# The layout of u's spectra in DRAM, the sign-flipped table, and the place of the table for the transform back

## The chip, the cores and the metric

The kernel runs on one core of a Trainium2 chip. The metric is the device time of one execution in microseconds (us), less is better. The core has five engines that run their own instruction lists and wait for each other by semaphores: TensorE (PE; its weight loads are listed as PEld), VectorE (DVE), ScalarE (ACT), GpSimd (POOL) and SyncE (SP), which here only issues transfers. Transfers between DRAM and the on-chip memory run on 16 DMA engines, whichever engine issued them.

## The reference

The whole is a conditioned layer for one sequence of 2,048 tokens and 512 channels, in float32. A vector c gives six rows of scales and shifts; a state-space convolution follows, then a token-shift mixer with an MLP.

```python
mod = (_silu(c) @ w_mod).reshape(c.shape[0], 6, 1, -1)
h = _layernorm(x, axis=-1) * (1 + ca) + sa
x = x + ga * _A_ref(h, ...)          # the convolution
h = _layernorm(x, axis=-1) * (1 + cb) + sb
x = x + gb * _B_ref(h, ...)          # token shifts and MLP

# _A_ref: taps K from the state space, then a causal convolution by a transform of length 4096
K = jnp.einsum("dn,dnl,dn->dl", Cc, P, dB).real
Kf = rfft2(pad(K)); Uf = rfft2(pad(u)); Yf = Uf * Kf
y = irfft2(Yf)[..., :L] + u * Dskip
```

The change touches the convolution alone: Uf, Kf, their product, and the first part of the transform back.

## The kernel before, in words

The work runs in three parts. The first, up to about 207 us of the profiled execution, makes the taps K (exponentials and sines on ACT, products on DVE, sums on PE) and beside it normalizes u and takes the first stage of u's transform, `u_dft` (lines 420 to 436). Each call makes 64 rows of half a spectrum for two token groups with the table `FU` as weights; ACT copies them to the tile `vs`, and SP stores them to `VU` in DRAM, 128 KB a store, in pieces of 256 floats (1 KB). There are 64 such stores.

The second part, from about 207 to 304 us, is the spectral one. `k_first` (eight rounds, with the table `FK` as moving operand) takes the first stage of the taps' transform. Then come sixteen steps, `steps` (line 1096): two halves of 256 channels (`jh`) by eight blocks of four of the 32 first-stage frequencies (`kc`). Each step has

- `load_vu` (line 638): SP loads 512 KB of VU to a tile `ld`, three steps ahead in the program; seven `ld` tiles are shared with the loads of w1 and ZT;
- `spectrum_u` (line 642): PE takes the second stage of u's transform with the table `TU`, ACT copies the result to `us`;
- `spectrum_k` (line 664): PE takes the second stage of the taps' transform, with parts of the table `T2`, and, for one of its four quarters, with the same table negated, the tile `T3`;
- `multiply` (line 685): DVE multiplies the two spectra;
- `back` (line 695): PE applies the table `Gm`, ACT copies to a tile `z` (two of them), and POOL stores z to `ZT` in DRAM, two transfers of 256 KB with 4-KB pieces.

`flip` (line 658) makes T3 on POOL: two operations for the eight frequencies that two steps need, into one of three tiles. The table `T2` stands in two tiles of sixteen frequencies, named xu in the profile, that were loaded at the end of the first part; `TU` stands in a tile named wm. Further loads stand in SP's queue among the VU loads: four of x (1 MB each), w1, FI, w2, and later the loads of ZT that the last stage of the transform back reads (`load_inv`, `inverse`). The third part, from about 304 us, is the rest of the transform back, the mixer and the MLP; PE is busy nearly throughout.

The order of each engine's work in the second part is the order in which the program's lines are written (`manual_schedule`). SP and POOL issue their transfers in that order, and an issue that has to wait holds back everything behind it on the same engine. A tile that takes the place of an older one waits for the last reader of the older one.

Of the kernel before, what the change touches and what calls it, by code (L numbers as in the profile page):

```python
# [7 lines left out]
F32 = mybir.dt.float32  # L8
# [3 lines left out]
OP = mybir.AluOpType  # L12
# [15 lines left out]
def shape_constants():  # L28
    f = lambda x: np.ascontiguousarray(x.astype(np.float32))
    k1, k2, q = np.arange(32), np.arange(64), np.arange(32)  # L30
    c2b = lambda c: np.where(c < 32, 31 - c, c)
    th = 2 * np.pi * (k1[None] + .5) * q[:, None] / 64
    W = np.stack([np.cos(th), -np.sin(th)], 1)
    Wt = W.transpose(0, 2, 1)
    FU = np.stack([np.stack([Wt, -Wt[..., ::-1]], 1), np.stack([Wt, Wt[..., ::-1]], 1)])
    FU = np.stack([FU, FU])
    FK = np.zeros((2, 2, 32, 2, 64))
    FK[:, 0, :, 0] = FK[:, 1, :, 1] = W.reshape(32, 64)
    b = c2b(np.arange(64))
    al = 2 * np.pi * b[:, None, None] * ((k1[None, :, None] + .5) / 4096 + k2[None, None, :] / 64)  # L40
    c, s = np.cos(al), np.sin(al)
    T2 = np.stack([np.stack([c, -s], 2), np.stack([s, c], 2)]).reshape(128, 32 * 128)
    be = np.arange(32) + .5
    al = 2 * np.pi * be[:, None, None] * ((k1[None, :, None] + .5) / 4096 + k2[None, None, :] / 64)
    TU = np.stack([np.cos(al), np.sin(al), np.cos(al), -np.sin(al)]).reshape(128, 32 * 64)
    al = 2 * np.pi * be[None, :] * k2[:, None] / 64
    cs = np.stack([np.cos(al), np.sin(al)], 2).reshape(64, 64)
    Gm = np.tile(np.concatenate([cs, cs], 1), (2, 1))
    sg = np.array([1.0, -1.0])[:, None]
    th = 2 * np.pi * (k1[:, None, None, None] + .5) * (sg * be[:, None, None] + 64 * q) / 4096  # L50
    FI = np.stack([np.cos(th), -sg * np.sin(th), -np.sin(th), -sg * np.cos(th)]) * (2 / 4096)
    eye = np.eye(16)
    j = np.arange(32)
    c0 = np.tile((eye[:, :, None] * (j + .5)).reshape(16, 512), (2, 1))
    C0 = np.zeros((2, 2, 32, 2, 512))
    C0[:, 0, :, 0], C0[:, 1, :, 1] = c0, c0
    C0 = C0.reshape(128, 1024)
    e1 = (eye[:, :, None] * j).reshape(16, 512)
    e2 = (eye[:, :, None] * np.ones(32)).reshape(16, 512)
    C1 = np.concatenate([e1, e1, e2, e2] * 2, 0)  # L60
    ex0 = np.concatenate([np.arange(31, -1, -1), np.arange(32, 64)])
    ex1 = np.concatenate([64 * np.arange(8), 512 * np.arange(4)])
    CE = np.concatenate([(eye[:, :, None] * ex0.reshape(2, 32)[:, None, None, :]).transpose(1, 0, 2, 3).reshape(16, -1),
                         np.zeros((16, 64 * NX1))], 1)
    CE = np.tile(CE, (8, 1))
    for u in range(4):
        CE[u * 32:u * 32 + 32, 1024 + u * 16 * NX1:1024 + (u + 1) * 16 * NX1] = \
            np.tile((eye[:, :, None] * ex1).reshape(16, -1), (2, 1))
    PA = np.zeros((2, 4, 16, 2, 2, 4, 2, 16))
    PB = np.zeros((4, 2, 16, 4, 4, 2, 4, 16))  # L70
    for e in range(16):
        for v in range(2):
            for u in range(4):
                for p in range(2):
                    PA[v, u, e, v, p, u, p, e] = 1
        for c in range(8):
            for p in range(4):
                PB[c // 2, c % 2, e, c // 4 * 2 + c % 2, p, 1 - c // 2 % 2, p, e] = 1
    return {k: f(v) for k, v in dict(
        FU=FU.reshape(128, 128), FK=FK.reshape(128, 128), T2=T2, TU=TU, G=Gm,  # L80
        FI=FI.reshape(128, 32 * 64), C0=C0, C1=C1, CE=CE, PA=PA.reshape(128, 512), PB=PB.reshape(128, 2048), ID=np.eye(128)).items()}
# [21 lines left out]
def dram(t, off, ap):  # L103
    return bass.AP(tensor=t.tensor, offset=t.offset + off, ap=ap)


def body(ctx, tc, A):
    nc = tc.nc
    V, S, P, T, Y = nc.vector, nc.scalar, nc.gpsimd, nc.tensor, nc.sync
# [7 lines left out]
    VU = dpool.tile([2, 64, 64, 256], F32, name="VU")  # L117
# [52 lines left out]
    pa12 = a12.enter_context(pool("a12"))  # L170
# [5 lines left out]
    FK = pa12.tile([128, 128], F32, name="FK")  # L176
# [8 lines left out]
    FU = ph.tile([128, 2, 64], F32, name="FU")  # L185
# [234 lines left out]
    def u_dft(b, eo):  # L420
        x = ut[b // 4]
        ps = [psu.tile([128, 512], F32, name="pu") for h in range(2)]
        for i in range(2):
            for h in range(2):
                j = slice(64 * h, 64 * h + 64)
                T.matmul(ps[h][i * 64:i * 64 + 64], FU[j, eo], x[j, b % 4 + i],  # L426
                         start=True, stop=True, skip_group_check=True)

        def evict():
            vs = uv.tile([128, 2, 512], F32, name="vs")  # L430
            for h in range(2):
                act(vs[:, h], ps[h])
                for i in range(2):
                    Y.dma_start(dram(VU, eo * 8192 + (h * 16 + b + i) * 256, [[16384, 64], [1048576, 2], [1, 256]]),
                                vs[i * 64:i * 64 + 64, h].rearrange("p (a d) -> p a d", a=2))
        later.append(evict)

# [166 lines left out]
    v0x = ExitStack()  # L604
    c2 = a2.enter_context(pool("c2"))
    TU = TU[0]
    Gm = c2.tile([128, 2, 64], F32, name="Gm")
    FI = c2.tile([128, 32, 2, 32], F32, name="FI")
    VK = [v0x.enter_context(pool("v0", side="right")).tile([128, 64, 2, 64], F32, name="VK0"),
          c2.tile([128, 64, 2, 64], F32, name="VK1")]  # L610
    ldp = a2.enter_context(pool("ldp", bufs=7))
    s2x = ExitStack()
    s2 = s2x.enter_context(pool("s2", bufs=2))
    psa = s2x.enter_context(pool("psa", bufs=2, space=PSUM))
    psb = s2x.enter_context(pool("psb", bufs=4, space=PSUM))
    kbank = lambda shape: psb.tile(shape, F32, name="pk2")
# [20 lines left out]

    def load_vu(jh, kc):
        t = vus[jh, kc] = block()
        Y.dma_start(t, dram(VU, jh * 1048576 + kc * 8 * 16384, [[256, 128], [32768, 4], [1, 256]]))  # L640

    def spectrum_u(jh, kc):
        vu = vus.pop((jh, kc))
        us = s2.tile([128, 3, 2, 256], F32, name="us")
        q = [psa.tile([128, 2, 256], F32, name="pk1") for ro in range(2)]
        for i in range(2):
            for kk in range(2):
                for ro in range(2):
                    r = slice(ro * 64, ro * 64 + 64)
                    T.matmul(q[ro][kk * 64:kk * 64 + 64, i], TU[r, kc * 4 + 2 * kk + i], vu[r, 2 * kk + i],  # L650
                             start=True, stop=True, skip_group_check=True)
        for n in range(3):
            act(us[:, n], q[n % 2])
        return us

    t3s = {}

    def flip(kc):
        t = t3s[kc] = c2.tile([128, 8, 64], F32, name="T3", bufs=3)
        for gh in range(2):  # L660
            r = slice(gh * 64, gh * 64 + 64)
            P.tensor_scalar(t[r], T2[kc // 4][r, kc % 4 * 4:kc % 4 * 4 + 8, 64 - gh * 64:128 - gh * 64], -1.0, None, op0=OP.mult)

    def spectrum_k(jh, kc):
        p = [kbank([128, 2, 2, 128]) for gh in range(2)]
        for i in range(2):
            for ro in range(2):
                for ri in range(2):
                    for kk in range(2):
                        for gh in range(2):  # L670
                            k1 = kc * 4 + 2 * kk + i
                            rows = slice(gh * 64, gh * 64 + 64)
                            w = T2[k1 // 16][rows, k1 % 16]
                            if ri == gh:
                                w = w[:, ro * 64:ro * 64 + 64]
                            elif ro == ri:
                                w = w[:, gh * 64:gh * 64 + 64]
                            else:
                                w = t3s[kc // 2 * 2][rows, k1 % 8]
                            T.matmul(p[gh][kk * 64:kk * 64 + 64, i, ro], w,  # L680
                                     VK[jh][rows, ri * 32 + k1].rearrange("p j g -> p (j g)"),
                                     start=(ri == 0), stop=(ri == 1), skip_group_check=True)
        return p
# [413 lines left out]
    with tc.manual_schedule():  # L1097
        load_vu(*steps[0])
        flip(0)
        Y.dma_start(Gm, A["G"].rearrange("p (a b) -> p a b", a=2))  # L1100
        for r in range(8):
            k_first(r)
            if r == 3:
                load_vu(*steps[1])
            if r == 6:
                load_vu(*steps[2])
        us = spectrum_u(*steps[0])
        split = None
        for n, st in enumerate(steps):
# [13 lines left out]
                us = spectrum_u(*steps[n + 1])  # L1123
            if n + 3 < 16:
                load_vu(*steps[n + 3])
            if n % 2 == 0 and n < 14:
                flip(steps[n + 2][1])
            if n in (3, 4, 6, 8):
                load_x(n - 3 if n < 5 else n // 2 - 1)
            if n == 9:  # L1130
# [171 lines left out]
```

## Time and profile before

| | |
|---|---|
| median of three runs | 689.6 us (687.0 to 690.3) |
| the profiled execution, its own time | 691.26 us |
| its span, first to last instruction | 689.5 us |
| mean granted TensorE clock | 0.989 |
| PE busy over the span | 642.6 us, 93% |
| DVE / ACT / POOL busy | 498.0 / 331.2 / 124.8 us |
| moved by the DMA engines | 86.42 MB, mean 125 GB/s |
| 16 loads of VU, 512 KB each | median 7.4 us from issue to landing |
| 30 stores of ZT by POOL, 256 KB each | median 6.2 us from issue to landing |

The profile comes from one execution. "Busy" counts the time in which an engine works, not the time in which it waits. A row `A <- B` in the waits says that A stood idle and that B ended it. The DMA share is the mean busy share of the 16 DMA engines; it can read slightly over 1 in a short window, since a packet counts where it starts. A landing is the time from a transfer's issue to its last byte.

### The profile page before, as it was taken

Reading aid. Unit: us, or ns where it says so; the run is one execution under the profiler, and the core shown is the slowest. Engines: PE = TensorE matmul, PEld = TensorE weight load, DVE = VectorE, ACT = ScalarE, POOL = GpSimd, SP = SyncE. Lnnn points to the kernel's source line nnn. Section 1 sums busy time; section 2 is a strip of 40 time slices with the busy share of each in tenths; the row PEclk is TensorE's granted clock in tenths of the full one; section 3 lists DMA queues with packets and bytes.
Section 4 is the critical chain, followed back from the end, with each engine's and each line's share of the span. In section 5 each row is a group of like instructions: output and inputs, shape, how many; then the busy total and the mean of one; then the engine's idle time right before and its main releaser. Section 6 shows DMA issues by size and latency. Waiting matters only on the chain.

```text
span 689.5 us, 16884 instructions
## 1 busy us (share of the span) xinstructions
PE 642.6 (93%) x7195; PEld 509.2 (74%) x7195; DVE 498.0 (72%) x795; ACT 331.2 (48%) x505; POOL 124.8 (18%) x236
## 2 busy tenths in 40 slices
PE   1899999999999998977998999999999999999996
PEld 0456655655569776634887889999899889898895
DVE  7899999999996887986987967464574536363522
ACT  3878988889875557432444623123131312222121
POOL 4011112112103355413741101001010000000000
PEclk9999999999999999998999999999999999999999
DMA  8603264643739997967387010020100201010001
GB/s 299 284 2 79 75 218 105 209 121 85 275 85 317 354 335 258 346 204 226 108 257 240 1 32 32 16 77 15 47 31 17 77 1 62 1 49 13 1 31 31
DMA packets 51091, 86.42 MB, mean 125 GB/s; under 512 B 4676, under 2 KB 39496, under 8 KB 48424
## 3 DMA queue, kind: packets, MB, share of 16 engines
q1 hardware_dynamic: 46712, 66.74, 30.1%
q0 software_dynamic: 3440, 17.57, 7.4%
q8 instruction: 56, 0.92, 0.6%
q10 hardware_dynamic: 864, 1.05, 0.5%
q14 instruction: 19, 0.16, 0.1%
HBM read 59.12 MB, written 32.90 MB: 133 GB/s over the span
## 4 chain that ended last, share of the span: by engine, by line
PE 70%; DVE 6%; DMA 5%; ACT 3%; POOL 2%; issue 1%; ACTq 0%; SPq 0%; DVEq 0%; POOLq 0%
PE pm L841 7%; PE pm L838 7%; PE pm L839 7%; PE xx L448 7%; PE pa L954 6%; PE pa L955 6%; PE pa L962 6%; PE kp L498 3%; DMA ZT<-z 3%; PE ph L893 2%; PE ph L895 2%; PE ph L892 2%; DMA ld<-ZT 2%; PE pu L426 2%; PE pT L803 2%; PE pk L626 2%
## 5 line engine op out<-in xcount | busy, mean ns | idle before, releaser
L115 ACT ACTIVATE gh<-pm 128x512 fp32r<-128x512 f32 (+1 forms) x48 | 26.9, 560 | 200.7 <-PE pm L841 200.7
L838 PE MATMUL pm<-nh,w3h 128*128 128x256 f32 (+1 forms) x352 | 86.6, 281 | 2.7 <-ACT nh L115 2.7
L839 PE MATMUL pm<-nh,w3l 128*128 128x256 f32 (+1 forms) x352 | 86.3, 280 | 0.1
L946 DVE TENSOR_TENSOR gl<-gf,gh 128x512 fp32r<-128x512 f32 (+1 forms) x48 | 30.8, 643 | 68.4 <-ACT gf L115 68.4
L954 PE MATMUL pa<-w4h,gh 128*128 128x512 f32 (+1 forms) x176 | 69.6, 395 | 0.0
L838 PEld LDWEIGHTS pm<-nh,w3h 128*128 128x128 f32 (+1 forms) x352 | 66.0, 187 | 4.4 <-ACT nh L115 2.9
L955 PE MATMUL pa<-w4l,gh 128*128 128x512 f32 (+1 forms) x176 | 68.9, 392 | 0.0
L839 PEld LDWEIGHTS pm<-nh,w3l 128*128 128x128 f32 (+1 forms) x352 | 65.9, 187 | 2.2 <-DVE w3l L756 0.5
L765 POOL TENSOR_TENSOR rs<-mv,eps_t 128x1 f32<-128x1 f32 (+1 forms) x39 | 11.0, 282 | 282.4 <-DVE mv L771 265.4
L841 PE MATMUL pm<-nl,w3h 128*128 128x256 f32 (+1 forms) x352 | 55.0, 278 | 0.0
L449 PE MATMUL xx<-MG,ON 64*128 64x512 f32 x160 | 48.1, 397 | 0.0
L962 PE MATMUL pa<-w4h,gl 128*128 128x512 f32 (+1 forms) x176 | 48.0, 390 | 0.0
L448 PE MATMUL xx<-MG,ON 64*128 64x512 f32 x160 | 48.0, 396 | 0.0
L841 PEld LDWEIGHTS pm<-nl,w3h 128*128 128x128 f32 (+1 forms) x352 | 47.0, 187 | 0.0
L898 DVE TENSOR_TENSOR h<-h,ph 128x512 f32<-128x512 f32 x16 | 11.0, 687 | 45.1 <-PE ph L895 45.1
L466 DVE SCALAR_TENSOR_TENSOR e<-tr,p 128x512 f32<-128x512 f32 x64 | 41.1, 684 | 1.5 <-ACT tr L115 1.5
L498 PEld LDWEIGHTS kp<-e,e 128*32 128x32 f32 x2048 | 30.1, 110 | 12.7 <-issue 7.6
L475 DVE TENSOR_TENSOR e<-tr,p 128x1024 f32<-128x1024 f32 x32 | 39.0, 1220 | 0.0
L476 DVE TENSOR_TENSOR e<-tr,m 128x1024 f32<-128x1024 f32 x32 | 39.0, 1219 | 0.0
L115 ACT ACTIVATE p<-xx 128x1024 f32<-128x1024 f32 (+1 forms) x40 | 37.5, 979 | 2.2 <-PE xx L252 1.0
L962 PEld LDWEIGHTS pa<-w4h,gl 128*128 128x128 f32 (+1 forms) x176 | 33.0, 188 | 7.3 <-DVE gl L946 0.2
L115 ACT ACTIVATE tr<-xx 128x1024 f32<-128x1024 f32 x32 | 33.0, 1030 | 9.6 <-PE xx L449 7.9
(236 smaller groups left out, 1731.6 us busy)
## 6 DMA issues: line engine op xcount, KB each, us to landing
VU<-vs SPq DMA_DIRECT2D x64, 128.0 KB, 3.7
ld<-VU SPq DMA_DIRECT2D x16, 512.0 KB, 7.4
ZT<-z POOLq DMA_DIRECT2D x30, 256.0 KB, 6.2
ld<-ZT SPq DMA_DIRECT2D x12, 512.0 KB
Dw<-in_w POOLq DMA_DIRECT2D x8, 688.0 KB, 4.7
xu<-in_u SPq DMA_DIRECT2D x4, 1024.0 KB, 8.0
KX<-in_x SPq DMA_DIRECT2D x4, 1024.0 KB, 8.0
GD<-go SPq DMA_DIRECT2D x16, 256.0 KB, 2.3
```

What stands on the lines that cost most here:

```text
L115: return S.activation(out, in_, f, bias=bias, scale=scale)
L448: T.matmul(x[:, :512], la, ma, start=(i == 0), stop=(i == len(ops) - 1))
L449: T.matmul(x[:, 512:], lb, mb, start=(i == 0), stop=(i == len(ops) - 1))
L466: V.scalar_tensor_tensor(e0[:, 1, a], tr[:, 1, 0], 1.0 - 2.0 * a, mg[:, a], op0=OP.mult, op1=OP.mult)
L475: V.tensor_mul(e0[:, 0], tr[:, 0, 0:1].to_broadcast([128, 2, 512]), mg)
L498: T.matmul(kp[32 * j:32 * j + 32, (k % 2) * 4 + g], e1[:, r, d], e0[:, r, :, d * 32:d * 32 + 32], start=(r == 0), stop=(r == 1), skip_grou ...
L838: T.matmul(p, wh[:, k, c], hi[k], start=(k == 0), stop=False)
L839: T.matmul(p, wl[:, k, c], hi[k], start=False, stop=False)
L841: T.matmul(p, wh[:, k, c], lo[k], start=False, stop=(k == 3))
L954: T.matmul(acc[i], gh[:m, e, s], W4h[:m, f], start=(f == 0), stop=False)
L955: T.matmul(acc[i], gh[:m, e, s], W4l[:m, f], start=False, stop=False)
L962: T.matmul(acc[i], gl[:m, e, s], W4h[:m, f], start=False, stop=(f == 10))
```

## The change

There are three edits.

**VU's layout.** It was [half of the channels][frequency and part][64 rows][256 channels], so that one row's neighbours in a block lay 128 KB apart, and a load took 512 pieces of 1 KB. It becomes [half][64 rows][part, frequency][256 channels]: a row's four frequencies of a block lie behind each other, and a load takes 128 pieces of 4 KB. For that the columns of the table `FU` are reordered from frequency-by-part to part-by-frequency. The store's pieces stay 1 KB; the 64 pieces of one store and half now lie behind each other. The same bytes move.

**The flipped table.** `flip` now negates one whole tile of T2 at a time, in four operations of the old size, into a T3 of all 32 frequencies that is kept; it is called twice, before the steps, and no longer in them.

**The table for the transform back.** `Gm` has no tile of its own any more: it is loaded into FK's, behind the first three VU loads in SP's queue, after the last round of `k_first`.

```diff
-    Wt = W.transpose(0, 2, 1)
-    FU = np.stack([np.stack([Wt, -Wt[..., ::-1]], 1), np.stack([Wt, Wt[..., ::-1]], 1)])
+    FU = np.stack([np.stack([W, -W[:, ::-1]], 1), np.stack([W, W[:, ::-1]], 1)])
...
-                    Y.dma_start(dram(VU, eo * 8192 + (h * 16 + b + i) * 256, [[16384, 64], [1048576, 2], [1, 256]]),
+                    Y.dma_start(dram(VU, (eo * 32 + h * 16 + b + i) * 16384, [[256, 64], [1048576, 2], [1, 256]]),
...
-    Gm = c2.tile([128, 2, 64], F32, name="Gm")
...
+    T3 = s2.tile([128, 32, 64], F32, name="T3", bufs=1)
...
     def load_vu(jh, kc):
         t = vus[jh, kc] = block()
-        Y.dma_start(t, dram(VU, jh * 1048576 + kc * 8 * 16384, [[256, 128], [32768, 4], [1, 256]]))
+        Y.dma_start(t.rearrange("p a d -> p (a d)"), dram(VU, jh * 1048576 + kc * 1024, [[8192, 2], [16384, 64], [1, 1024]]))
...
-    t3s = {}
-
-    def flip(kc):
-        t = t3s[kc] = c2.tile([128, 8, 64], F32, name="T3", bufs=3)
+    def flip(i):
         for gh in range(2):
             r = slice(gh * 64, gh * 64 + 64)
-            P.tensor_scalar(t[r], T2[kc // 4][r, kc % 4 * 4:kc % 4 * 4 + 8, 64 - gh * 64:128 - gh * 64], -1.0, None, op0=OP.mult)
+            for a in range(0, 16, 8):
+                P.tensor_scalar(T3[r, i * 16 + a:i * 16 + a + 8], T2[i][r, a:a + 8, 64 - gh * 64:128 - gh * 64], -1.0, None, op0=OP.mult)
...
-                                w = t3s[kc // 2 * 2][rows, k1 % 8]
+                                w = T3[rows, k1]
...
         load_vu(*steps[0])
         flip(0)
-        Y.dma_start(Gm, A["G"].rearrange("p (a b) -> p a b", a=2))
+        flip(1)
         for r in range(8):
             k_first(r)
             if r == 3:
                 load_vu(*steps[1])
             if r == 6:
                 load_vu(*steps[2])
+        Gm = pa12.tile([128, 2, 64], F32, name="FK")
+        Y.dma_start(Gm, A["G"].rearrange("p (a b) -> p a b", a=2))
...
-            if n % 2 == 0 and n < 14:
-                flip(steps[n + 2][1])
```

In `dram(VU, offset, pattern)` the pattern lists [step, count] from the outermost dimension to the innermost, in floats.

On SP, at the start of the spectral part, the transfers stood so before (`ld<-VU` is a VU load, `KX<-in_x` a load of x; a name behind "waits" that begins with DMAHW is an earlier transfer, PE_49 is TensorE):

```order
L1100 DMA Gm<-in_G 128x128
L640 DMA ld<-VU 128x4x256 [waits DMAHW6_49]
L640 DMA ld<-VU 128x4x256 x4
L640 DMA ld<-VU 128x4x256 [waits DMAHW3_49]
L724 DMA KX<-in_x 128x2048 [waits DMAHW4_49,PE_49]
L640 DMA ld<-VU 128x4x256 [waits DMAHW5_49,PE_49]
```

and stand so now:

```order
L639 DMA ld<-VU 128x1x1024
L639 DMA ld<-VU 128x1x1024 [waits DMAHW6_49]
L1105 DMA FK<-in_G 128x128 [waits PE_49]
L639 DMA ld<-VU 128x1x1024 x3
L639 DMA ld<-VU 128x1x1024 [waits DMAHW3_49]
L721 DMA KX<-in_x 128x2048 [waits DMAHW4_49]
```

The load of G has moved behind the third VU load and waits for TensorE; four more VU loads and the first load of x stand behind it. A VU load's shape on the tile's side is 128 rows of one run of 1,024 floats, where it was 128 rows of four runs of 256.

On POOL, in the spectral part, the table's operations (`T<-xu`) and the stores of ZT stood so before:

```order
L662 TENSOR_SCALAR T_3081<-xu 64x512 x2
L662 TENSOR_SCALAR T_3355<-xu 64x512 x2
L706 DMA ZT_61<-z 32x2x1024 x4
L662 TENSOR_SCALAR T_3500<-xu 64x512 x2
L706 DMA ZT_61<-z 32x2x1024 x4
L662 TENSOR_SCALAR T_3646<-xu 64x512 x2
```

and stand so now:

```order
L511 DMA Dw_64<-in_w 16x8192 x2
L659 TENSOR_SCALAR T_3070<-xu 64x512 x8
L703 DMA ZT_61<-z 32x2x1024 x16
L703 DMA ZT_62<-z 32x2x1024 x14
L762 TENSOR_TENSOR rs_79<-mv_78,eps_t 128x1
```

All eight operations stand ahead of the first store, and no table operation stands among the stores.

## The prediction

> **What bounds the kernel now.** I read the busy times by stretch first, to find what runs where the change acts, then the chain of waits and the waits there, then SP's queue and the DMA packets. The windows are the transform of the kernel's taps, the sixteen spectral steps, and the hand-over behind them (start and end, then busy time of PE, PEld, DVE, ACT, POOL, then TensorE clock, DMA share, GB/s):
>
> ```profile
> 213.00:224.00 11.00, 10.67 (x190) 10.56 (x190) 8.00 (x12) 8.16 (x15) 2.43 (x2) 1.00 0.91 291
> 224.00:304.00 80.00, 72.85 (x1528) 52.97 (x1526) 69.60 (x116) 45.73 (x90) 35.15 (x42) 1.00 0.91 312
> 304.00:316.00 12.00, 5.22 (x47) 2.82 (x47) 3.70 (x9) 0.34 (x1) 0.00 (x0) 0.85 0.76 231
> ```
>
> Sixteen steps in 80 us are 5.0 us a step. PE is busy 91% of that, DVE 87%, the 16 DMA engines 91%: three resources near their end together, so whatever takes a DMA engine much longer shows at once. The chain of waits names what ends last in it (start, length, what):
>
> ```profile
> 234.17 8.87 DMA ZT<-z
> 252.91 8.02 DMA ZT<-z
> 291.66 7.89 DMA ld<-ZT
> ```
>
> and the waits from 200 to 310 us (engine, line, waited for: sum, times, longest):
>
> ```profile
> ACT z L115 <- DMA ZT<-z: 8.7, 3, 4.3
> PEld pk L680 <- POOL T L662: 2.3, 3, 0.8
> PE pk L680 <- POOL T L662: 1.6, 3, 0.5
> ```
>
> Nobody waits for a VU load: `ld` has seven buffers, and SP's queue runs far ahead, as its timeline shows:
>
> ```profile
> 212.65 0.39 SPq L640 DMA_DIRECT2D ld<-VU  x1
> 213.09 1.61 SPq L1100 DMA_DIRECT2D Gm<-in_G  x1
> 214.74 5.15 SPq L640 DMA_DIRECT2D ld<-VU  x6
> 220.00 1.67 SPq L724 DMA_DIRECT2D KX<-in_x  x1
> ```
>
> What is to be priced is therefore DMA engine time. Packets, MB and share of all 16 engines, first over 217 to 225 us (VU loads alone, 1-KB packets), then 226 to 228 us (an x load, 8-KB packets), then the stage's two queues:
>
> ```profile
> DMA packets 2822, 2.82 MB, mean 352 GB/s; under 512 B 80, under 2 KB 2821, under 8 KB 2821
> q1 hardware_dynamic: 2821, 2.80, 106.2%
> ...
> DMA packets 168, 0.82 MB, mean 409 GB/s; under 512 B 6, under 2 KB 77, under 8 KB 77
> q1 hardware_dynamic: 168, 0.82, 101.5%
> ...
> q1 hardware_dynamic: 11422, 16.88, 61.8%
> q0 software_dynamic: 2400, 7.87, 28.2%
> ```
>
> A 1-KB packet costs 1.062 x 16 x 8 us / 2,741 = 50 ns on one engine (the 80 tiny ones cost next to nothing). The 8-KB window gives 1.015 x 16 x 2 / 0.82 MB = 39.6 us per MB on one engine, so 162 ns for 4 KB. The ZT stores are 4-KB packets: 0.282 x 16 x 80 us / 1,920 (7.87 MB in 4 KB) = 188 ns. A 4-KB piece of VU lies between; I take 162, since the x load is a read as the VU load is.
>
> **Over how many engines a transfer is spread.** Packets under 512 B are the end marks. The 217 to 225 window has 2,741 pieces and 80 marks, 15 for 512 pieces (its edges cut loads): 16 for each load. From 12.5 to 15.0 us four one-row loads, DS, pass, beside one POOL load that ends:
>
> ```profile
> DMA packets 196, 1.09 MB, mean 434 GB/s; under 512 B 20, under 2 KB 24, under 8 KB 105
> ```
>
> 24 - 20 = 4 pieces of 512 B are the DS rows; of the 20 marks 16 belong to the POOL load and 4 to the rows: one each. So a transfer has one mark for each engine it used, and one row uses one engine. SP's large loads and stores of before begin their pattern, on both sides, with a count that is a multiple of 16 (128, 96, 64 or 32). The changed VU load begins its DRAM side with a count of **2**: `[[8192, 2], [16384, 64], [1, 1024]]`. The 2 and the 64 cannot fold into one count of 128, as 64 x 16384 is not 8192. Two readings fit the trace: engines by the first count (two here), or by the number of pieces (128, so sixteen). The one-row loads do not part them. I take the first: a split by the first count explains each mark, and no transfer of before is seen to be split along a second count.
>
> [...]
>
> **The change part by part.**
>
> *The VU load.* On sixteen engines it costs 512 x 50 ns / 16 = 1.60 us now, and would cost 128 x 162 / 16 = 1.30 us. On two it is 64 x 162 ns = **10.4 us**, against a step of 5.0. Sixteen of them are 166 us on those two engines (at 188 ns, 193 us). It cannot hide: it is two stages long.
>
> *What shares these two engines.* SP's queue is in order on each engine, so the other loads stand between the VU loads. Ahead of the last VU load are x (4 MB), FI, w1 (1 MB each), the first four ZT loads (2 MB) and G: 8.45 million bytes, 0.53 MB an engine; at 39.6 to 46.9 us per MB (the stage's q1 row: 0.618 x 16 x 80 / 16.88) 21 to 25 us, say 22. The ZT stores come on POOL's queue, 8 packets an engine a step: 13 steps x 8 x 188 ns = 19 us. Sum: 166 + 22 + 19 = 207 us from 212.65, so the last VU load lands at about **420 us**.
>
> *What waits for it.* The last VU load feeds the matmuls that began at 293.78; the second four loads of the first ZT half (2 MB), with w2 (1 MB) ahead of them, stand behind it: 0.2 MB an engine, 9 us, and 3 us for two more steps' stores; landed at 432. Before, the matmuls that need them began at 299.59, after a wait of 1.48:
>
> ```profile
> 293.78 1.04 PE L650 MATMUL pk<-ld,wm 64*64 64x256 f32 x16
> 299.59 1.93 PE L731 MATMUL pk<-ld,FI 128*32 128x256 f32 x32 [1.48 <-DMA ld<-ZT]
> ```
>
> PE is in order, so the last step's transform back stands behind these: 432 - 299.6 = 132 us later. From there nothing reads VU, and all transfers start with 64 or more: the rest keeps its length.
>
> *The flipped table.* Sixteen POOL operations become eight, all at the start:
>
> ```profile
> L662 POOL TENSOR_SCALAR T<-xu 64x512 f32<-64x512 f32 x16 | 24.6, 1536 | 27.3 <-DMA wm<-in_TU 26.2
> ```
>
> 8 x 1.54 = 12.3 us from about 209.3 end near 222, before the first spectral step's matmuls at 225; step 0 needs the first three. The second half waits for the second T2 load, there at 212.8. PE's waits for T (2.3 and 1.6 us, the same three events) go: at most 2 us, worth nothing where PE waits for VU.
>
> *G in FK's place.* SP's queue now stops at G until the last FK matmul, at 224.4, with four VU loads and x behind it. On two engines that is covered: the three VU loads ahead last 31 us, to 244. With sixteen it is not: 1.5 MB are through by about 218.5, and the DMA engines idle 6 us, 2.1 MB at 351 GB/s that then press into a stage whose free DMA time is 0.09 x 80 = 7 us. Price there: 0 to 6 us.
>
> *VU stores and the reordered FU:* 1-KB pieces and a first count of 64 as before; only their addresses close up. Nothing waits for them but the first VU load.
>
> The sum is made against the profiled execution's own 691.3 us (span 689.5), 1.7 above the runs' median: 691.3 + 132 = 823, less 1 to 2 for the table's waits: **822 us**.
>
> **Rivals.**
>
> 1. *Sixteen engines after all, not slower.* Place: the DMA engines in the stage. 0.30 us a load off (0.11 at 188 ns), 1.8 to 4.8 over sixteen, and up to 2 for the table, with G's 6 us sunk into the free 7. Time: 685 to 688. For it: the 8.7 us ACT waits for ZT stores shrink with shorter queues. Against: the first count of 2.
> 2. *Sixteen engines, and G's wait decides.* The 2.1 MB held back meet the first ZT stores, which already take 8.87 us and hold ACT. It decides if the ZT stores' delay exceeds the 1.8 to 4.8 us saved: 691 + 6 - 3 = 694.
> 3. *Two engines, but dearer.* If the two are slowed as ZT stores are (188 ns, +27 us) and 1-KB traffic delays them more, 850 to 875. If the ZT stores and other loads slip beside the VU packets, the sum is 212.65 + 166 + 12: 795.
>
> A load decides as soon as its time exceeds the step: 20.7 us of engine time over fewer than about five engines.
>
> **How the numbers follow.** Two engines, 0.86 (0.78 within the sum's bounds, 785 to 875, with 0.08 beyond), rival 1 0.08, rival 2 0.06. A measurement of this kernel can tell 0.5%, 3.4 us, from no change. Faster: rival 1's better half and a little more, 0.06; same: the rest of it and half of rival 2, 0.07; slower: 0.87. The range 785 to 875 leaves the sixteen-engine cases out, and holds 0.78.
>
> **What would show it.** In the changed profile: VU loads landing in over 10 us, tens of them when queued; 224 to 304 at a DMA share near 0.4 or below; the chain from 224 to about 430 mostly "DMA ld<-VU"; PE, DVE and ACT idle half of each step at a pitch of 12 to 13 us; each VU load with 2 marks instead of 16; after the stage the old lengths. The forecast is wrong if these loads land in 5 to 8 us with a DMA share near 0.9; then rivals 1 and 2 part by whether SP's gap from 214 to 224 is followed by longer waits of ACT z for ZT.

## The result, and the profile after

The changed kernel takes **827.6 us** (median of four runs, 825.0 to 828.3), against 689.4 us (687.0 to 690.3) for the kernel before on the same chip: a ratio of 1.200, 95% interval 1.196 to 1.205. Its profiled execution has a span of 825.6 us, at a mean granted TensorE clock of 0.919. Times are medians of all runs, while each ratio is of the fast runs alone, which leaves out two of the twelve runs of one experiment (the doubled stores). The same bytes move, and PE, DVE and ACT run as many instructions as before; nearly all of the 138 us is waiting.

The stretches of the changed kernel's trace show where (start and end, length, then busy time of PE, PEld, DVE, ACT and POOL, TensorE clock, DMA share, GB/s):

```profile
213.00:224.00 11.00, 10.87 (x192) 10.67 (x192) 7.67 (x12) 7.86 (x15) 6.09 (x5) 1.00 0.13 48
224.00:304.00 80.00, 39.51 (x608) 29.71 (x608) 26.42 (x43) 18.03 (x34) 6.53 (x12) 0.73 0.35 108
304.00:440.00 136.00, 61.93 (x916) 38.75 (x920) 43.32 (x72) 28.53 (x55) 9.61 (x18) 0.71 0.46 139
```

From 224 to 304 us, where the kernel before ran all sixteen steps, PE is now busy for half of the time and the DMA engines for 35%. By these averages nothing is near its end, and yet the stage lasts to 440. In the first row VU loads run nearly alone, at a share of 0.13. The packets of 214 to 231 us say the same more closely (packets, MB, share of all 16 engines):

```profile
DMA packets 207, 0.87 MB, mean 51 GB/s; under 512 B 2, under 2 KB 2, under 8 KB 204
q1 hardware_dynamic: 204, 0.83, 12.1%
```

12.1% of sixteen engines is 1.94 engines. With 202 pieces of 4 KB in 17 us, a piece costs 0.121 x 16 x 17 / 202 = 163 ns on its engine, and the load moves at 51 GB/s. The end marks agree: over the whole execution, packets under 512 B fell from the first of these rows (the page of before) to the second (the page of after).

```profile
DMA packets 51091, 86.42 MB, mean 125 GB/s; under 512 B 4676, under 2 KB 39496, under 8 KB 48424
```

```profile
DMA packets 44723, 86.42 MB, mean 105 GB/s; under 512 B 4452, under 2 KB 31080, under 8 KB 42056
```

4,676 - 4,452 = 224 = 16 loads x 14: each VU load leaves 2 marks where it left 16.

The chain of waits in the stage (start, length, what) and the waits from 205 to 460 us (sum, times, longest):

```profile
253.81 39.55 DMA ld<-VU
...
295.05 37.84 DMA ld<-VU
...
392.98 18.89 DMA ld<-VU
...
439.81 0.60 ACT z L114
```

```profile
PE pk L649 <- DMA ld<-VU: 88.7, 14, 11.8
```

Three loads of VU alone make up 96 us of the chain; PE waits for fourteen of the sixteen. The last of these three lands at 411.9 and is the fifteenth load. The sixteenth landed at about 425.0, as PE's matmuls on it show (first row below). PE reaches the matmuls behind the last ZT loads at 434.57 (second row), where the kernel before reached them at 299.59:

```profile
425.15 1.98 PE L649 MATMUL pk<-ld,wm 64*64 64x256 f32 x16 [6.07 <-DMA ld<-VU]
...
434.57 2.89 PE L728 MATMUL pk<-ld,FI 128*32 128x256 f32 x32 [4.07 <-DMA ld<-ZT]
```

The copy to z behind it starts at 439.81 (the chain above); in the chain of the kernel before the same copy reads

```profile
303.75 0.60 ACT z L115
```

From there to the end of the span are 385.8 us in both kernels (825.6 - 439.8, and 689.5 - 303.75).

SP's queue holds something that the prediction had not asked about. In the timeline of its issues (start, busy time, line, what, how many), and in the summary of the loads' line (shortest, median and longest issue in ns):

```profile
212.08 10.29 SPq L639 DMA_DIRECT2D ld<-VU  x3
223.93 8.42 SPq L1105 DMA_DIRECT2D FK<-in_G  x1
232.40 32.51 SPq L639 DMA_DIRECT2D ld<-VU  x4
...
410.56 16.17 SPq L718 DMA_DIRECT2D ld<-ZT  x4
...
L639 SPq DMA_DIRECT2D ld<-VU x16: 514/3186/11854, 212.1 to 394.4; - x16
```

Before, the same summary read

```profile
L640 SPq DMA_DIRECT2D ld<-VU x16: 359/377/2106, 212.6 to 278.7; - x16
```

An issue of a VU load took 0.38 us; now the median is 3.2 us and the longest 11.9. While the two engines are behind, the issue itself takes long, and G, a 64-KB transfer, takes 8.4 us to be issued behind three of these loads.

### The profile page after: what moved, and what is told of

It reads as the page before. It is cut to its first block, busy times and chain, and to the rows that moved or that the text cites. A ratio compares the mean times of both kernels' runs of the same rounds, so it can differ in the third digit from the quotient of the medians.

```text
span 825.6 us, 16875 instructions
## 1 busy us (share of the span) xinstructions
PE 669.0 (81%) x7195; PEld 524.2 (63%) x7195; DVE 498.1 (60%) x795; ACT 332.2 (40%) x505; POOL 111.6 (14%) x228
## 2 busy tenths in 40 slices
DMA packets 44723, 86.42 MB, mean 105 GB/s; under 512 B 4452, under 2 KB 31080, under 8 KB 42056
## 4 chain that ended last, share of the span: by engine, by line
PE 56%; DMA 19%; DVE 11%; SPq 7%; ACT 3%; issue 2%; POOL 1%; ACTq 0%; DVEq 0%; POOLq 0%
DMA ld<-VU 12%; PE pm L838 6%; PE pm L836 6%; PE pm L835 6%; PE xx L447 6%; PE pa L951 5%; PE pa L952 5%; PE pa L959 5%; SPq L639 3%; PE kp L497 3%; DMA ld<-in_w 2%; DMA ld<-ZT 2%; PE ph L890 2%; PE ph L892 2%; PE ph L889 2%
## 5 line engine op out<-in xcount | busy, mean ns | idle before, releaser
L649 PE MATMUL pk<-ld,wm 64*64 64x256 f32 x256 | 30.8, 624 | 90.6 <-DMA ld<-VU 88.7
L649 PEld LDWEIGHTS pk<-ld,wm 64*64 64x64 f32 x256 | 14.1, 208 | 109.7 <-issue 108.6
L687 DVE TENSOR_TENSOR ma<-pk,us 128x512 f32<-128x512 f32 x32 | 21.9, 685 | 81.0 <-PE pk L677 81.0
L114 ACT ACTIVATE us<-pk 128x512 f32<-128x512 f32 x48 | 25.2, 599 | 93.6 <-issue 80.9
L762 POOL TENSOR_TENSOR rs<-mv,eps_t 128x1 f32<-128x1 f32 (+1 forms) x39 | 10.9, 280 | 286.2 <-DVE mv L768 265.6
L677 PEld LDWEIGHTS pk<-VK,xu 64*64 64x64 f32 x768 | 44.8, 187 | 5.1 <-issue 4.1
L448 PE MATMUL xx<-MG,ON 64*128 64x512 f32 x160 | 47.1, 389 | 0.0
L447 PE MATMUL xx<-MG,ON 64*128 64x512 f32 x160 | 47.0, 389 | 0.0
L677 PE MATMUL pk<-VK,xu 64*64 64x128 f32 x768 | 45.4, 346 | 0.0
L703 POOL DMA_DIRECT2D ZT<-z x30 | 16.1, 542 | 196.6 <-ACT z L114 196.6
```

Of the source, the lines that this page charges most:

```text
L114: return S.activation(out, in_, f, bias=bias, scale=scale)
L447: T.matmul(x[:, :512], la, ma, start=(i == 0), stop=(i == len(ops) - 1))
L448: T.matmul(x[:, 512:], lb, mb, start=(i == 0), stop=(i == len(ops) - 1))
L677: T.matmul(p[gh][kk * 64:kk * 64 + 64, i, ro], w, VK[jh][rows, ri * 32 + k1].rearrange("p j g -> p (j g)"), start=(ri == 0), stop=(ri == 1 ...
```

## The experiments

The theory: a transfer is spread over no more DMA engines than the first count of its DRAM pattern allows; a first count of 2 puts each VU load on two engines, and that is all of the loss. The rivals: the edits that move SP's queue (G's wait) or POOL's work (the whole flipped table) have a part in it; or the 4-KB pieces at their new addresses are dear by themselves. Every kernel below computes the whole output. The runs of before beside them had medians of 688.8 to 689.8 us, and each ratio is against those beside it.

### The load as two transfers, each with a first count of 64

```diff
-        Y.dma_start(t.rearrange("p a d -> p (a d)"), dram(VU, jh * 1048576 + kc * 1024, [[8192, 2], [16384, 64], [1, 1024]]))
+        for ri in range(2):
+            Y.dma_start(t[ri * 64:ri * 64 + 64].rearrange("p a d -> p (a d)"),
+                        dram(VU, jh * 1048576 + ri * 8192 + kc * 1024, [[16384, 64], [1, 1024]]))
```

> The changed kernel with each VU load made as two transfers, one for each half of the tile's partitions, so that the DRAM pattern begins with 64 instead of 2. Same bytes, same addresses, same 4-KB pieces, 32 issues instead of 16. Theory (a transfer is spread over as many DMA engines as its first count allows, 2 in the change): all sixteen engines again, the VU loads cost 1.3 to 1.5 us of all engines each, and the time falls back to 684 to 694 us. Rival (the 4-KB pieces at a 64-KB pitch in DRAM, or the load of G that holds SP's queue, cost the 136 us): these are untouched, so it stays at 815 to 830 us.

Measured: 699.8 us (698.3 to 705.9), 1.0153 of before (1.0139 to 1.0167). Same layout, same pieces, same addresses, and 128 us are gone. What changed is the first count, and that a load is now two transfers over half of the partitions each; the next experiment keeps the half loads and varies the count. But 10.5 us stay, and the expected range is missed by 6. The profiled execution was the longest of the six (705.9 us), so its trace shows more than the usual loss. The stretch of this kernel's sixteen steps, the packets of 213 to 219 us and the wait for ZT stores from 205 to 330 us:

```profile
224.00:304.00 80.00, 66.22 (x1384) 50.79 (x1380) 59.05 (x99) 38.91 (x77) 14.05 (x26) 0.96 0.98 302
...
DMA packets 397, 1.35 MB, mean 225 GB/s; under 512 B 71, under 2 KB 71, under 8 KB 394
q1 hardware_dynamic: 396, 1.34, 89.7%
...
ACT z L114 <- DMA ZT<-z: 18.4, 5, 5.5
```

The DMA engines are now full (0.98 against 0.91) and move less (302 against 312 GB/s). A 4-KB piece costs 0.897 x 16 x 6 / 325 = 265 ns, not 162 (the 71 marks are left out: in the traces of before and after the record of a mark lasts 9 ns). ACT's wait for the ZT stores has grown from 8.7 to 18.4 us.

### First counts of 4 and of 8

The 64 rows in DRAM got a gap of 4 KB after every 16 (or 8) rows, so that they no longer lie at one pitch, and each half load begins its pattern with 4 (or 8). The edit for four (VU's larger size is not shown):

```diff
...
-                    Y.dma_start(dram(VU, (eo * 32 + h * 16 + b + i) * 16384, [[256, 64], [1048576, 2], [1, 256]]),
+                    Y.dma_start(dram(VU, (eo * 32 + h * 16 + b + i) * 16384 + (eo * 32 + h * 16 + b + i) // 16 * 1024, [[256, 64], [1052672, 2], [1, 256]]),
...
-        Y.dma_start(t.rearrange("p a d -> p (a d)"), dram(VU, jh * 1048576 + kc * 1024, [[8192, 2], [16384, 64], [1, 1024]]))
+        for ri in range(2):
+            Y.dma_start(t[ri * 64:ri * 64 + 64].rearrange("p a d -> p (a d)"),
+                        dram(VU, jh * 1052672 + ri * 8192 + kc * 1024, [[263168, 4], [16384, 16], [1, 1024]]))
```

> As the kernel with half loads, but VU's rows lie in groups of 16 with 4 KB of padding behind each group, so that a half load's pattern begins with a count of 4. Theory: four engines; a load is 32 pieces an engine, 5.3 us; the last VU load lands at 212.7 + 16 x 5.3 + 41 = 338 us, the last ZT loads 12 us later, 50 us after the 299.6 of before: 735 to 750 us. Rival (the number of pieces sets the engines, 64 pieces give sixteen): the time of the half loads, 684 to 694 us.

> The same with groups of 8 rows: a half load's pattern begins with 8. Theory: eight engines, 16 pieces an engine and load, 2.6 us; the last VU load lands at about 212.7 + 42 + 41 = 296 us, with the ZT loads behind it at 307, 7 us after before: 693 to 702 us. Rival (number of pieces): 684 to 694 us.

Measured: 749.7 us with four (1.0881, 1.0852 to 1.0910), 714.3 us with eight (1.0386, 1.0338 to 1.0434). The loads' queue from 213 to 219 us, first with four, then with eight:

```profile
DMA packets 143, 0.57 MB, mean 94 GB/s; under 512 B 9, under 2 KB 9, under 8 KB 141
q1 hardware_dynamic: 141, 0.54, 24.8%
```

```profile
DMA packets 212, 0.82 MB, mean 136 GB/s; under 512 B 20, under 2 KB 20, under 8 KB 207
q1 hardware_dynamic: 210, 0.79, 44.2%
```

24.8% is 4 of 16 engines, 44.2% is 7 of 16. The end marks say it exactly. Over the whole execution the packets under 512 B are 4,452 in the changed kernel (16 loads), and with 32 half loads 4,548 with four, 4,676 with eight and 4,932 with a first count of 64. That is 4,420, and 2, 4, 8 and 16 more for each load or half load; before, with a first count of 128, it was 4,676, which is 16 for each of the sixteen loads. The windows of 213 to 219 us, whose edges cut loads, have 4.4, 6.7 and, with 64, 14.0 marks for 64 pieces. So in these runs the number of engines follows the first count of the DRAM pattern: 2, 4 and 8 engines with counts of 2, 4 and 8, sixteen with 64 and 128. The tile's side began with 128 or 64 in all these kernels, so these runs don't show what a small count there does. Four came out at the upper end of its range; eight came out 12 us above it. The rows say why. A piece costs 0.248 x 96 / 132 = 180 ns with four engines and 0.442 x 96 / 190 = 223 ns with eight, and I had taken the 162 of the full-width load. (The profiled execution with eight took 721.6 us, the longest of its four.) With these prices, which the runs gave afterwards, one sum covers the doses. An engine that carries VU pieces also carries, in each step, eight ZT pieces at 188 ns (1.5 us) and a sixteenth of the prediction's 22 us of other loads (1.4 us), 2.9 us together by this estimate:

| engines | pieces on each, per load | ns a piece | us a step, with the 2.9 | 16 x the excess over 5.0 | measured |
|---|---|---|---|---|---|
| 2 | 64 | 163 | 13.3 | +133 | +138 |
| 4 | 32 | 180 | 8.7 | +59 | +61 |
| 8 | 16 | 223 | 6.5 | +24 | +27 |
| 16, two half loads | 8 | 265 | 5.0 | 0 | +10.5 |
| 16, before | 32 of 1 KB | 50 | 4.5 | under | 0 |

The last column is the ratio less one, times the 689 us of before. The 13.3 us a step can be seen in the trace too: from the first VU load's issue to the sixteenth's landing are (425.0 - 212.1) / 16 = 13.3. The row of the half loads is the one that the sum does not give: it stands just at the step, at a DMA share of 0.98, and still costs 10 us.

### Half loads with the kernel before's layout

This raises the question whether half loads are dear by themselves. So the kernel before, with its 1-KB pieces, got its loads split in the same way and nothing else.

```diff
-        Y.dma_start(t, dram(VU, jh * 1048576 + kc * 8 * 16384, [[256, 128], [32768, 4], [1, 256]]))
+        for ri in range(2):
+            Y.dma_start(t[ri * 64:ri * 64 + 64], dram(VU, jh * 1048576 + kc * 8 * 16384 + ri * 16384, [[256, 64], [32768, 4], [1, 256]]))
```

> The kernel before with nothing changed but each VU load made as two transfers of 64 partitions, 1-KB pieces. Theory (half the partitions move at a lower rate): a 1-KB piece costs some 65 ns instead of 50, a load 2.0 us instead of 1.6, 7 us of DMA time over sixteen loads in a stage that is 91% full: 692 to 700 us. Rival (two transfers move as fast as one, and the 4-KB pieces were to blame): 688 to 691 us.

Measured: 700.2 us (696.9 to 701.5), 1.0138 (1.0119 to 1.0158), at the upper end of the range. Half loads are dear by themselves. Its two stretches, to be read beside those of the kernel before, and ACT's wait for the ZT stores from 205 to 330 us:

```profile
213.00:224.00 11.00, 11.00 (x196) 10.88 (x200) 7.61 (x11) 7.87 (x14) 1.13 (x1) 1.00 0.98 223
224.00:304.00 80.00, 66.78 (x1450) 51.16 (x1451) 62.11 (x103) 42.15 (x82) 33.67 (x40) 0.98 1.01 300
...
ACT z L115 <- DMA ZT<-z: 7.7, 3, 4.8
```

In the first row the DMA engines are full (0.98) and move 223 GB/s, where the whole loads moved 291 at a share of 0.91. So what the first experiment left is for the most part not a matter of the new layout: a load of 64 partitions keeps all sixteen engines busy for longer than a whole load needs for the same bytes. ACT's wait for the ZT stores is no measure of this loss: it is 7.7 us here, against 8.7 before and 18.4 in the first experiment.

With half loads the DMA engines moved 223 and 238 GB/s from 213 to 224 us (here and in the next experiment), with whole ones 352 and 390 from 217 to 225 us (in the kernel before and in the second run of whole 4-KB loads), at DMA shares of 0.98 to 1.07. Whether the lower rate comes from the 64 partitions or from two transfers in the place of one, no run here shows.

### G's wait, with half loads

SP's queue stops at G until the last FK matmul. Here four more VU loads are issued ahead of G.

```diff
+        for st in steps[3:7]:
+            load_vu(*st)
         Gm = pa12.tile([128, 2, 64], F32, name="FK")
...
-            if n + 3 < 16:
+            if 7 <= n + 3 < 16:
```

> As the kernel with half loads, but the VU loads of steps 3 to 6 are issued ahead of the load of G, as they ran before the change; only x, and what follows, stands behind G's wait for TensorE. If G's wait costs what it holds back (2.1 MB pushed into the stage), this is 2 to 6 us faster than the half loads with G ahead; if the stage's free DMA time swallows it, the two are equal within 1 us.

Measured: 697.1 us (695.6 to 697.8), 1.0115 (1.0101 to 1.0129), so 2.7 us less than with G's wait; that is part of the 10.5. SP's queue and the stretch before the steps, with the wait still ahead of the loads (first experiment), then without it:

```profile
211.95 4.33 SPq L640 DMA_DIRECT2D ld<-VU  x6
223.80 0.33 SPq L1107 DMA_DIRECT2D FK<-in_G  x1
...
213.00:224.00 11.00, 11.00 (x200) 10.82 (x202) 7.80 (x12) 7.87 (x15) 5.97 (x5) 1.00 0.60 147
```

```profile
211.58 10.14 SPq L640 DMA_DIRECT2D ld<-VU  x14
223.43 0.33 SPq L1109 DMA_DIRECT2D FK<-in_G  x1
...
213.00:224.00 11.00, 11.00 (x200) 10.68 (x199) 8.18 (x12) 7.86 (x14) 5.94 (x5) 1.00 1.03 238
```

The gap is filled (share 0.60 to 1.03), and where the DMA engines are full behind it, that is worth about 2.7 us (the two ratios are each known to 1 us).

### The other two edits alone

The kernel before with the whole flipped table and with G in FK's place, but with VU's old layout, store and load (and its columns of FU, not shown).

```diff
...
-                    Y.dma_start(dram(VU, (eo * 32 + h * 16 + b + i) * 16384, [[256, 64], [1048576, 2], [1, 256]]),
+                    Y.dma_start(dram(VU, eo * 8192 + (h * 16 + b + i) * 256, [[16384, 64], [1048576, 2], [1, 256]]),
...
-        Y.dma_start(t.rearrange("p a d -> p (a d)"), dram(VU, jh * 1048576 + kc * 1024, [[8192, 2], [16384, 64], [1, 1024]]))
+        Y.dma_start(t, dram(VU, jh * 1048576 + kc * 8 * 16384, [[256, 128], [32768, 4], [1, 256]]))
```

> The change without its VU part: layout, FU and load as before; the table negated once and whole, G loaded into FK's place. The price of these two edits alone: up to 2 us off for PE's waits for the table, 0 to 6 us on for what G's wait holds back: 687 to 694 us. If they were the reason why the half loads stayed 11 us slower, this is 697 us or more.

Measured: 690.2 us (688.2 to 691.9, twelve runs), 1.0000 (0.9986 to 1.0014). Beside the old layout the two edits together do nothing that can be measured; neither was run alone, so two small effects of opposite sign are not excluded. So the loss comes with the new layout and its load.

### Whole loads of 128 rows with 4-KB pieces

What would the 4-KB pieces bring if the load kept all sixteen engines and all 128 partitions? With VU as [half][part][row][frequency], a load is one pattern of 128 rows. The store's pattern would then need four counts, and it is written as two stores of 64 KB. (FU keeps the columns of before, not shown here.)

```diff
...
-                    Y.dma_start(dram(VU, (eo * 32 + h * 16 + b + i) * 16384, [[256, 64], [1048576, 2], [1, 256]]),
-                                vs[i * 64:i * 64 + 64, h].rearrange("p (a d) -> p a d", a=2))
+                    for a in range(2):
+                        Y.dma_start(dram(VU, a * 1048576 + (eo * 32 + h * 16 + b + i) * 8192, [[256, 32], [524288, 2], [1, 256]]),
+                                    vs[i * 64:i * 64 + 64, h, a * 256:a * 256 + 256])
...
-        Y.dma_start(t.rearrange("p a d -> p (a d)"), dram(VU, jh * 1048576 + kc * 1024, [[8192, 2], [16384, 64], [1, 1024]]))
+        Y.dma_start(t.rearrange("p a d -> p (a d)"), dram(VU, jh * 1048576 + kc * 1024, [[8192, 128], [1, 1024]]))
```

> The changed kernel with VU laid out as [half of channels][part][row][frequency], so that a load is one transfer of 128 rows at one pitch (the DRAM pattern begins with 128), of 4-KB pieces; for that each store of VU becomes two of 64 KB, 128 in all, and FU keeps the column order of before. Flipped table and G as in the change. Theory: the half loads were still 11 us slower than before because a transfer into 64 partitions runs at about 240 GB/s (1.43 MB in 6 us at a full DMA share) where one into 128 runs at 350 or more; with 128 rows a load costs 1.3 us of all engines and the time is 686 to 693 us. Rival (what is left comes from G's wait and the table, not from the half-width loads): 697 to 702 us, as the half loads.

The second run adds the four loads ahead of G:

> The same, with the VU loads of steps 3 to 6 issued ahead of the load of G. If G's wait costs as in the half loads (699.8 against 697.1), this is 2 to 4 us below the kernel of 128-row loads, and then 683 to 690 us, at or below before. If with faster loads the stage's free DMA time takes it up, the two are within 1 us of each other.

Measured: 694.4 us (691.5 to 700.6), 1.0073 (1.0044 to 1.0101); with the loads ahead of G 695.6 us (694.0 to 696.4), 1.0080 (1.0068 to 1.0092). Both ranges were missed by one and by six us. G's wait is not the reason, since taking it away brought nothing. Nor are the pieces: the packets of 217 to 225 us in the second run, where VU loads run alone,

```profile
DMA packets 861, 3.12 MB, mean 390 GB/s; under 512 B 103, under 2 KB 103, under 8 KB 857
q1 hardware_dynamic: 860, 3.11, 99.7%
```

give 0.997 x 16 x 8 / 757 = 169 ns a piece and 390 GB/s, against 352 for the 1-KB pieces of before. The load did become cheaper, and the time did not.

The first run's chain shows where its time went; below it stand the stretch from 213 to 224 us and the matmul at which PE had to wait:

```profile
210.46 3.33 DMA VU<-vs
214.25 0.61 ACT VK L115
...
228.59 1.02 PE pk L651 x16
...
213.00:224.00 11.00, 9.10 (x114) 9.10 (x116) 4.15 (x6) 5.66 (x10) 5.96 (x5) 0.69 0.65 239
...
214.91 0.58 PE L627 MATMUL pk<-FK,KX 64*128 64x128 f32 x1 [3.20 <-ACT VK L115]
```

The first copy to VK now waits for the last store of VU and starts at 214.25 (212.81 before); PE idles 3.2 us for it, its granted clock reads 0.69 from 213 to 224, and the eight rounds of `k_first` end at 228.59 instead of 224.43: 4.2 us later, 1.4 of it from the late copy and 2.7 from rounds that take longer (14.3 us instead of 11.6). From there the steps take as long as before: the chain's copy to z starts 79.7 us after that point, where it was 79.3. So in this trace nearly the whole loss lies ahead of the steps, and the cheaper loads gain nothing in them. Nor do they shorten ACT's wait for the ZT stores, which is 13.9 us from 205 to 330, against 8.7 before.

### The doubled stores

Two runs asked whether the doubled stores make that entry late. In the first the kernel before gets only these.

```diff
-                    Y.dma_start(dram(VU, eo * 8192 + (h * 16 + b + i) * 256, [[16384, 64], [1048576, 2], [1, 256]]),
-                                vs[i * 64:i * 64 + 64, h].rearrange("p (a d) -> p a d", a=2))
+                    for a in range(2):
+                        Y.dma_start(dram(VU, a * 1048576 + eo * 8192 + (h * 16 + b + i) * 256, [[16384, 64], [1, 256]]),
+                                    vs[i * 64:i * 64 + 64, h, a * 256:a * 256 + 256])
```

> The kernel before with one edit: each of the 64 stores of u's spectra is written as two stores, one per half of the channels, with the same pieces of 1 KB and the same addresses; the loads are untouched. The run with 128-row loads of 4-KB pieces had to split its stores in the same way, and its trace shows the queue on SyncE busy issuing stores up to 212, the first spectrum's eviction waiting for the last store, and the first product ending at 228.6 instead of 224.4. If the doubled stores are what cost that run its 5 us, this run is 3 to 6 us slower than before: 692 to 696 us. If the 4-KB loads themselves cost it, this run is within 2 us of before: 688 to 692 us.

Measured: 693.2 us (689.8 to 702.6, twelve runs), 1.0048 (1.0026 to 1.0071): 3.3 us slower, with an interval of 1.8 to 4.9. By themselves the doubled stores thus cost most of what the run with whole 4-KB loads lost, 5.0 us (3.0 to 7.0). In its profiled execution, which was one of its shortest (690.1 us), the entry is late by 1.0 us, and the clock did not fall:

```profile
205.50 5.56 SPq L435 DMA_DIRECT2D VU<-vs  x8
211.17 1.30 SPq L534 DMA_DIRECT2D xu<-in_T  x1
...
214.47 0.37 PE L627 MATMUL pk<-FK,KX 64*128 64x128 f32 x1 [2.71 <-ACT VK L115]
```

```profile
210.46 2.90 DMA VU<-vs
213.83 0.60 ACT VK L115
...
303.49 0.60 ACT z L115
```

The same place in the kernel before:

```profile
204.72 2.57 SPq L434 DMA_DIRECT2D VU<-vs  x4
207.39 0.54 SPq L533 DMA_DIRECT2D xu<-in_T  x1
```

SP needs 5.6 us to issue the last eight stores, where four took 2.6, and the load of T2 goes out at 211.2 instead of 207.4. But by the copy to z that late entry is made up: it starts at 303.49, against 303.75 in the kernel before. So the timed runs show that the doubled stores cost 3.3 us, and this profile shows what they delay; where the 3.3 us arise is not shown.

The other run is the one with whole 4-KB loads, with four of the last eight stores issued from ACT.

```diff
-                        Y.dma_start(dram(VU, a * 1048576 + (eo * 32 + h * 16 + b + i) * 8192, [[256, 32], [524288, 2], [1, 256]]),
+                        q = S if a and eo and b == 14 else Y
+                        q.dma_start(dram(VU, a * 1048576 + (eo * 32 + h * 16 + b + i) * 8192, [[256, 32], [524288, 2], [1, 256]]),
```

> As the run with 128-row loads of 4-KB pieces (694.4 us), but of the last eight of its 128 stores four are issued from ScalarE's queue, where ScalarE stands idle. If the issue of the stores on SyncE's queue held the stage's start, its start moves forward by some 2.5 to 4 us: 689 to 692.5 us, no different from before or slower by up to 0.5%. If it isn't the issue, it stays at 693 to 696 us.

Measured: 694.3 us (693.1 to 699.4), 1.0080 (1.0051 to 1.0110): no gain. ACT's timeline says why this did not test what it was meant to:

```profile
204.18 1.60 ACTq L436 DMA_DIRECT2D VU<-vs  x2
205.83 0.60 ACT L115 ACTIVATE vs<-pu 128x512 f32<-128x512 f32 x1 [1.68 <-DMA VU<-vs]
206.82 2.66 ACTq L436 DMA_DIRECT2D VU<-vs  x2
209.53 0.60 ACT L115 ACTIVATE KX<-kp 128x512 f32<-128x512 f32 x1 [3.11 <-DMA VU<-vs]
215.46 2.56 ACT L115 ACTIVATE VK<-pk 128x512 f32<-128x512 f32 x5 [5.33 <-DMA VU<-vs]
```

The issues took ACT's time and held its second copy to vs by 1.7 us and KX by 3.1; the last store went out later, and VK starts at 215.46, not sooner. In this trace the clock stays at 1.00 from 213 to 224, and the rounds end at 227.10, 1.5 us sooner than in the first run of whole loads; the medians are equal even so. How much of the remaining 1.7 us (5.0 less 3.3, no more than the two intervals leave open) is something else stays open. No version tried here beats the kernel before.

## Why the prediction was right

The forecast was 822 us with a range of 785 to 875; the time is 827.6. Point by point:

- **Two engines, by the first count of the DRAM pattern.** Right, and it was the choice between two readings that the profile of before did not part. The share of 0.121, the two end marks a load and the dose at 4, 8 and 64 show it; rivals 1 and 2 rested on sixteen engines and fall.
- **162 ns a piece, 10.4 us a load.** Right where it was used: 163 ns. The two bounds, the x load and the ZT store, were 162 and 188, and the read was the better one.
- **166 + 22 + 19 = 207, the last VU load at 420.** It landed at 425.0, 213 us after the first was issued. The loads make 16 x 64 x 163 ns = 167 of that, so what else held the two engines took 46 us and not 41.
- **Last ZT loads at 432, 132 us later than before.** PE began behind them at 434.57, 135 later; its 32 matmuls there took 2.89 us instead of 1.93, so that the copy to z came 136 later. That the end came so near is partly luck: the last VU load was 5 us late, and from its landing to PE's start were 9.6 us, where 9 for the loads behind it and 3 for stores had been summed. What I had left out is SP's own time: it took 16.2 us, until 426.73, to issue the four ZT loads. Here that added nothing to the sum that can be seen, since PE did not wait longer behind the VU load than had been summed.
- **Less 1 to 2 for the table's waits.** This should not have been taken off: the prediction itself had called these waits worth nothing where PE waits for VU.
- **From there the old lengths.** Right: 385.8 us in both. (Not all transfers there start with 64 or more, as the prediction has it: the stores of ZT start with 32, in both kernels.)
- **The flipped table hidden, done near 222.** It ended at 220.4, as POOL's rows show:

```profile
207.09 6.09 POOL L659 TENSOR_SCALAR T<-xu 64x512 f32<-64x512 f32 x4 [25.01 <-PE kp L497]
214.31 6.05 POOL L659 TENSOR_SCALAR T<-xu 64x512 f32<-64x512 f32 x4 [1.14 <-DMA xu<-in_T]
```

  With G moved as well it is worth 0.0 us (-1.0 to +1.0).
- **G's wait, 0 to 6 us on sixteen engines.** 2.7 us with half loads, whose DMA engines are full; nothing that can be measured beside the flipped table, or with whole 4-KB loads. In the changed kernel the two engines are busy throughout (12.1% of sixteen from 214 to 231 us), and it is G that takes 8.4 us to be issued.
- **The pitch.** 12 to 13 us were expected; it was 13.3.
- **The bounds of the rivals.** Two sums of the prediction do not come out. The case of rival 3 in which other traffic slips beside the VU packets is 212.65 + 166 + 12 = 391, 91 us after 299.6, so 782 and not 795: below the range. And rival 1's 0.11 us a load at 188 ns is 0.10. Neither entered the forecast.

Two steps were wrong without moving the forecast. "A load decides as soon as its time exceeds the step: 20.7 us of engine time over fewer than about five engines" is refuted by eight engines, which cost 27 us: by the sum in the table the step has to hold all that an engine carries in it, 2.9 us of other traffic included, and the piece grows to 223 ns. And rival 1 gave 685 to 688 us to sixteen engines, from cheaper loads. The whole loads did become cheaper (169 ns for 4 KB, 390 GB/s), yet no run gained. The doubled stores' 3.3 us do not hide it by the ratios, as 1.7 us of loss remain beside them. The loads were not what the steps waited for, as the prediction's own waits had shown, and ACT's wait for the ZT stores, which rival 1 wanted to see shrink, grew from 8.7 to 13.9.

## What to carry to other kernels

Before a transfer's pattern is rewritten for larger pieces, read the first count of its DRAM side: here first counts of 2, 4 and 8 left a load on 2, 4 and 8 of the sixteen engines and cost 138, 61 and 27 us. The bytes moved did not show it (86.42 MB before and after); the DMA share of a stretch where the loads ran nearly alone did (12.1%, 24.8% and 44.2%), and so did the end marks. Compare the time of everything one DMA engine carries in a step, not that of one load, with the step. And price the other side of a layout: stores that had to be split to suit the load cost 3.3 us here with the same bytes and pieces.

## What the runs showed of the hardware that was not expected

- **An issue takes long when few engines are fed.** With loads on two engines, one issue on SP took up to 11.9 us (median 3.2, against 0.38 before), and a 64-KB load that stood behind three of them took 8.4 us to issue. With half loads on four engines it was up to 6.7 us (median 1.4), with eight 1.6 (0.58) and with sixteen 1.6 (0.59). The four loads of x, behind and among the loads on two engines, took 4.6 to 11.3 us to issue, against 0.5 to 1.7 before. Nor does a transfer on sixteen engines pass by on the two: 112 of G's 128 pieces, with 14 marks, ran from 232 to 234 us, and the other 16 only between 243 and 247 us, behind the third VU load. So here a load on few engines delayed later transfers of its queue, also those on all sixteen.
- **Half loads cost engine time.** In half loads a 4-KB piece took 180 ns with four engines, 223 with eight and 265 with sixteen, against 169 in whole loads over 128 partitions on sixteen. Splitting each of the sixteen loads into two halves cost the kernel before 9.5 us (8.2 to 10.9).
- **The granted TensorE clock fell where PE waited.** It was 0.71 to 0.73 over the slow stage, against 1.00 in the same steps before, though PE ran fewer matmuls there (608 from 224 to 304 us, against 1,528 before); and 0.69 from 213 to 224 us in the first two runs of whole loads, around waits of 3.2 and 3.5 us, though it stayed at 1.00 around waits of 2.7 and 3.0 us in the two runs on the doubled stores. Behind the wait of 3.2 us the rounds of `k_first` took 2.7 us longer. What sets it, these runs do not show.
